# Fused window attention and gated FFN on one core: products with v in every third batch, a new order of the start, 30 heap slots

## The chip, the cores and the metric

The kernel runs on one core of one Trainium2 chip. The metric is the device time of the whole program in microseconds (us); lower is better. TensorE multiplies matrices, VectorE and ScalarE work element by element (both read PSUM), GpSimd works element by element on SBUF only, SyncE (SP) issues nearly all the DMAs.

## The reference

```python
xn = layernorm(x)                                  # x: 2048 tokens x 512
q, k, v = split(xn @ wqkv)                         # 32 heads of 16
scores = einsum("qd,kd->qk", q, k) * 16**-0.5
mask: 0 <= i - j < 256                             # causal, window of 256
o = softmax(scores, masked) @ v
s = o.reshape(S, D) @ wo
h = silu(xn @ w1) * (xn @ w3)                      # F = 1792
g = silu(h @ w2)
return x + s * g
```

All inputs are float32. The weights are large, so scores have a wide range, and the kernel carries about float32 accuracy through.

## The kernel before, in words

**Numbers.** A float32 matrix product is made of three float16 products: each operand is scaled by a power of two and cut into a high part (a cast) and a low part (the rest), and hi*hi + lo*hi + hi*lo is summed in PSUM. For tokens these parts are `XH` and `XL`; for weights `split` makes them (ScalarE the high part, VectorE the low) or `split_pool` (ScalarE twice, GpSimd the low part in two halves). The power of two of a weight comes from its sum of squares: `squares` adds them up per partition (on ScalarE for the first `on_act` parts, on VectorE for the rest; both write the squares themselves into a scratch tile that nobody reads), and `powers` sums over the partitions by a small matmul with ones and rounds on VectorE.

**Tiles and stages.** The tokens go in four tiles of 512 (`t`), the heads in four groups of eight (`g`). `prepare(0)` loads four blocks of x, takes mean and variance (`stats`), the inverse root by Newton steps (`rstd`), centres them, and turns each by four transposes on TensorE (`turn`: PSUM to XH by ScalarE, to XL by VectorE one step later). `project(t, g, k)` makes q (k = 0) or k (k = 1) for a group: twelve matmuls of 128x512 in two halves of six, then out to DRAM, from where `fetch` brings it back with one head to a strip of partitions. `value(j)` makes v for a block of 128 tokens.

**Attention** is done in 32 units `(t, g, p)`, four heads each. `pass1` makes the scores once with the queries on the partitions (L459) and takes the row maximum on VectorE (L464); at its end the maxima are turned on TensorE (L475), go to DRAM and come back as two more rows of the q operand. `pass2`, two units later in the order of the program, makes the scores again with the keys on the partitions (L506, maximum already subtracted), adds the masks on VectorE (L515, L520), takes the exponential on ScalarE into a tile `pt` (L524) and multiplies with v in float32 (L534; each such product appears as two instructions in the trace) into the one PSUM tile `po`. A unit has six chunks of keys and queries (five in the first tile).

**The order.** TensorE runs in the order in which the program is written; on the other engines a scheduler orders at compile time, and `tc.issue_after` keeps what is written in its block behind a given instruction of the same engine. `batches(u, ahead)` pairs the scores of unit u with the first pass of the unit two further on: seven batches of one or two score tiles. Products with v are not made with their scores but put on a list, `late`, and taken off in a later batch: `take_cols` says in which. `spread` puts dense work (FFN, projections, v, the output product) between the batches by matmul counts; `later(n, f)` runs f after n such steps. `flush` runs what is still queued. The FFN is written as a list of pieces (`feed_forward`): `load` brings raw weights, `measure` and `measure_down` scale and cut them during the first tile (cut weights are kept in DRAM and fetched again for later tiles), `gate_up` (L667) and `down` (L712) multiply.

**Memory.** Most passing tiles of 2 KB a partition are slots of one heap: `take` gives the slot that has been free longest, `give` puts it back, in program order; the writer of a slot waits for the last user of what was in it. The heap has 33 slots. PSUM has three buffers for dense results (`psm`), two double-size ones for scores (`pss`), one for `po`.

**The start** is written out by hand: fillers on TensorE (`keep_busy`), the statistics, the scale of the first q and k weights between the turns, then the projections of groups 0 and 1, v, and the scale and cut of the next weights between them. The fourth q and k weights are loaded (`qk[3][0]`) before the first unit, their squares are asked for after it (`qk[3][1]`), their scale three steps later.

**The end**: four calls of `total`, each the output product of 128 tokens (twelve matmuls), gated, added to x and stored.

Of the kernel before, what the change touches and what calls it, by code (L numbers as in the profile page):

```python
# [28 lines left out]
NT = 4  # L29
# [18 lines left out]
SLOTS = 33  # L48
# [13 lines left out]
def tile_block(ctx: ExitStack, tc: tile.TileContext, x, wqkv, wo, w1, w3, w2, out):  # L62
# [98 lines left out]
    ones = const.tile([4, KW], F16, name="ones")  # L161
# [6 lines left out]
    def squares(parts, on_act=0, apart=0):  # L168
# [4 lines left out]
        def one(i, raw):  # L173
            sq = take(BF16)
            if i < on_act:
                nc.scalar.activation(sq[:, 0:raw.shape[-1]], raw, AF.Square, accum_out=ssq[:, i:i + 1])
            else:
                nc.vector.tensor_tensor_reduce(out=sq[:, 0:raw.shape[-1]], in0=raw, in1=raw, scale=1.0, scalar=0.0,
                                               op0=ALU.mult, op1=ALU.add, accum_out=ssq[:, i:i + 1])
            give(sq)  # L180
# [35 lines left out]
    def split(hi, lo, raw, s):  # L216
        nc.scalar.activation(hi, raw, AF.Copy, scale=s)  # L217
# [16 lines left out]
    def weights(name, w):  # L234
# [8 lines left out]
        def norm(apart=0):  # L243
            cell["sb"] = squares(cell["raw"], on_act=4 * (name == "wv"), apart=apart)
# [22 lines left out]
    def weights_qk(g):  # L267
# [11 lines left out]
        def scale():  # L279
# [3 lines left out]
            cell["sw"] = scaled(inv, WS, f"sw{g}")  # L283

            cell["es"] = es = const.tile([P, 1], F32, name=f"es{g}")
            nc.vector.tensor_scalar(es, p2, p2, DH**-0.5 / QS**2, op0=ALU.mult, op1=ALU.mult)

        def cut():
            hi = const.tile([P, 2, NC, P], F16, name=f"whi{g}")
            lo = const.tile([P, 2, NC, P], F16, name=f"wlo{g}")  # L290
            for k, raw in enumerate(cell["raw"]):
                split(hi[:, k].rearrange("p c f -> p (c f)"), lo[:, k].rearrange("p c f -> p (c f)"), raw, cell["sw"])
            give(*cell["raw"])
            WQK[g] = hi, lo, cell["es"]
# [8 lines left out]
    def prepare(t):  # L303
# [3 lines left out]
        xts = {}  # L307

        def load(b):
            xts[b] = take(F32)  # L310
            nc.sync.dma_start(xts[b], x[t * TW + b * P:t * TW + (b + 1) * P, :])
# [20 lines left out]
        def centre(b):  # L332
            nc.vector.tensor_scalar(xts[b], xts[b], mv[:, b, 0:1], rs[:, b:b + 1], op0=ALU.subtract, op1=ALU.mult)

        def turn(b):
# [4 lines left out]
            pt = psm.tile([P, NC, P], F32, name="mm", tag="mm")  # L340
# [3 lines left out]
            with urgent():  # L344
                nc.scalar.copy(xh[:, :, c], pt)
# [48 lines left out]
    def project(t, g, k):  # L394
# [3 lines left out]
        def part(half):  # L398
# [3 lines left out]
            if half == 0:  # L402
                cell["pp"] = psm.tile([P, TW], F32, name="mm", tag="mm")
            for c in (2 * half, 2 * half + 1):
                for i, (a, b) in enumerate(((hi, xh), (lo, xh), (hi, xl))):
                    nc.tensor.matmul(cell["pp"], a[:, k, c, :], b[:, c, :], start=c == 0 and i == 0,  # L406
                                     stop=c == NC - 1 and i == 2)
            if half == 0:
# [20 lines left out]
        return [(6, lambda h=h: part(h)) for h in range(2)]  # L429
# [59 lines left out]
    def pass2(t, g, p):  # L489
# [6 lines left out]
        def scores(c):  # L496
# [25 lines left out]
            cell[c] = pt = ppool.tile([P, 4, 256], F32, name="pt")  # L522
# [85 lines left out]
    def measure(f, apart=0):  # L608

        raws = [RAW[f + i][0] for i in range(2)]  # L610
        sb = squares([raws[0][0], raws[1][0], raws[0][1], raws[1][1], RAW[f][1], RAW[f + 1][1]], on_act=6 if f == 0 else 4, apart=apart)
# [154 lines left out]

    def feed_forward():
# [47 lines left out]
    def batches(u, ahead):  # L815
# [10 lines left out]
        for k, pair in enumerate(pairs):  # L826
            take_cols = not ahead or (k and k % 2 == 0 if u else k == 1)
# [13 lines left out]
            made.append((COLS * 2 * take_cols if u else 0, batch))  # L841
# [30 lines left out]
    nc.vector.memset(ones, ONE)  # L872
# [46 lines left out]
    with tc.issue_after(lasts["cut"].ins):  # L919
# [108 lines left out]
```

## Time and profile before

| | us |
|---|---|
| median of 3 runs | 888.89 (888.86 to 893.99) |
| the profiled execution | 888.72 |
| its span, first to last instruction | 886.7 |
| TensorE busy | 851.2 (96%) |
| VectorE busy | 620.3 (70%) |
| ScalarE busy | 442.2 (50%) |
| GpSimd busy | 193.9 (22%) |
| mean granted TensorE clock | 0.993 |
| HBM traffic over the span | 118 GB/s |

PE is TensorE's matmuls, PEld its weight loads, DVE VectorE, ACT ScalarE, POOL GpSimd, SPq SyncE's queue. A row of the chain in time or of the timeline is: start, length, engine, line, operation, tile written <- tiles read, shapes, number merged, and in brackets the idle time of the engine before it with what ended it. A row of groups is: line, engine, operation, tiles, shapes, count | busy us, mean ns | idle us before, by what. A row of waits is: who waited for whom: us in total, times, longest. A row of stages is: window, length, busy us and count of each engine (PE, PEld, DVE, ACT, POOL), granted clock, DMA share, GB/s.

### The profile page before, as it was taken

How to read it: one execution, taken by the hardware profiler on the slowest of the kernel's cores; microseconds unless marked ns; L12 is line 12 of the kernel's file. 1: busy time of each engine (PE TensorE's matmuls, PEld its weight loads, DVE VectorE, ACT ScalarE, POOL GpSimd, SP SyncE). 2: the span in 40 equal slices, each digit the busy share in tenths (PEclk: the TensorE clock that was granted, in tenths of full speed). 3: DMA queues.
4: the chain of work that ended last, by engine and by line, in shares of the span. 5: the costliest groups of instructions: out<-in, count | busy, mean ns of one | idle time of the engine just before them, and what ended most of it. 6: DMA issues, size and time to landing. Idle time of an engine off the chain costs nothing.

```text
span 886.7 us, 20405 instructions
## 1 busy us (share of the span) xinstructions
PE 851.2 (96%) x7813; PEld 376.8 (42%) x7813; DVE 620.3 (70%) x1823; ACT 442.2 (50%) x657; POOL 193.9 (22%) x308
## 2 busy tenths in 40 slices
PE   8978998899999999999999999999999999999997
PEld 3433443444444444444444444444444444444443
DVE  6766967786767667778767776677667777676435
ACT  6776867473435444444444454444454444544521
POOL 1236236151111203111111111221111103131211
PEclk9999999999999999999999999999999999999999
DMA  9827734636643343451434334433442343422201
GB/s 289 240 85 231 225 112 128 209 109 196 167 132 84 102 125 96 131 158 52 145 102 119 106 91 131 131 102 90 136 123 59 107 133 114 116 92 85 63 11 57
DMA packets 94989, 110.51 MB, mean 125 GB/s; under 512 B 16956, under 2 KB 60076, under 8 KB 94892
## 3 DMA queue, kind: packets, MB, share of 16 engines
q1 hardware_dynamic: 94892, 109.21, 41.7%
q8 instruction: 61, 1.00, 0.5%
q14 instruction: 36, 0.29, 0.1%
HBM read 76.28 MB, written 28.57 MB: 118 GB/s over the span
## 4 chain that ended last, share of the span: by engine, by line
PE 65%; DVE 9%; issue 7%; DMA 6%; ACT 6%; SPq 4%; POOL 4%; POOLq 0%; DVEq 0%; ACTq 0%
PE mm L667 22%; PE mm L712 14%; PE po L534 8%; PE s L506 5%; PE mm L406 5%; PE mm L754 4%; PE s L459 3%; POOL slot L223 3%; DVE junk L464 3%; PE mm L380 3%; SPq L573 2%; ACT pt L524 1%; ACT slot L227 1%; DMA slot<-in_B_w_dram 1%; DMA dW<-slot 1%
## 5 line engine op out<-in xcount | busy, mean ns | idle before, releaser
L524 ACT ACTIVATE pt<-s,es 128x1024 f32<-128x1024 f32 (+1 forms) x184 | 200.8, 1093 | 233.0 <-DVE s L520 119.9
L667 PE MATMUL mm<-XH,slot 128*128 128x512 f16 x896 | 269.4, 382 | 2.1 <-DVE XL L350 1.2
L223 POOL TENSOR_TENSOR slot<-slot,slot 128x256 f16<-128x256 f32 (+1 forms) x220 | 147.4, 695 | 537.6 <-ACT slot L691 414.7
L464 DVE CUSTOM_DVE_ANT_0 junk<-s,MW 128x320 bf16<-128x320 f32 x448 | 217.8, 486 | 23.9 <-PE s L459 13.5
L667 PEld LDWEIGHTS <-slot 128*128 128x128 f16 x1344 | 122.0, 98 | 162.8 <-issue 32.2
L667 PE MATMUL mm<-XL,slot 128*128 128x512 f16 x448 | 170.8, 381 | 0.0
L712 PE MATMUL mm<-slot,slot 128*128 128x512 f16 x672 | 159.1, 380 | 0.3
L520 DVE TENSOR_TENSOR s<-s,M 128x512 f32<-128x512 f32 x128 | 89.0, 696 | 80.3 <-PE s L506 74.4
L534 PE MATMUL po<-pt,V 128*32 128x128 f32 (+1 forms) x1920 | 99.1, 333 | 0.0
L712 PEld LDWEIGHTS <-slot 128*128 128x128 f16 x672 | 60.7, 98 | 80.1 <-issue 12.9
L459 PE MATMUL s<-KA,qa 48*64 48x320 f16 (+2 forms) x1024 | 73.2, 297 | 11.4 <-DVE M L464 7.7
L506 PE MATMUL s<-qa,KA 50*64 50x128 f16 (+1 forms) x1920 | 74.2, 251 | 7.6 <-DVE M L464 4.6
L515 DVE TENSOR_TENSOR s<-s,M 128x1024 f32<-128x1024 f32 x56 | 68.8, 1228 | 17.0 <-PE s L506 14.7
L506 PEld LDWEIGHTS <-KA 50*64 50x64 f16 x1920 | 33.5, 105 | 82.3 <-issue 49.2
L682 DVE SCALAR_TENSOR_TENSOR slot<-slot,mm 128x512 f32<-128x512 f32 x56 | 38.4, 685 | 40.2 <-ACT slot L678 40.2
L691 ACT CAST slot<-slot 128x512 f16<-128x512 f32 x56 | 34.5, 616 | 54.5 <-DVE slot L687 54.5
L534 PEld LDWEIGHTS po<-pt,V 128*32 128x32 f32 x1920 | 50.2, 110 | 25.1 <-issue 12.4
L678 ACT ACTIVATE slot<-mm,sgs 128x512 f32<-128x512 f32 x56 | 38.2, 683 | 28.5 <-PE mm L667 28.2
L687 DVE SCALAR_TENSOR_TENSOR slot<-mm,slot 128x512 f32<-128x512 f32 x56 | 38.6, 689 | 18.7 <-PE mm L667 18.6
L728 DVE SCALAR_TENSOR_TENSOR slot<-mm,dsc,slot 128x512 f32<-128x512 f32 x48 | 35.9, 749 | 21.8 <-PE mm L712 21.7
L223 POOL TENSOR_TENSOR on<-on,rb 128x256 f32<-128x256 f32 x32 | 22.6, 727 | 126.5 <-DMA qa<-dm 92.5
L406 PE MATMUL mm<-XH,whi 128*128 128x512 f16 x128 | 49.2, 384 | 0.6 <-ACT whi L217 0.6
(111 smaller groups left out, 834.7 us busy)
## 6 DMA issues: line engine op xcount, KB each, us to landing
slot<-dW SPq DMA_DIRECT2D x126, 256.0 KB
slot<-in_B_w_dram SPq DMA_DIRECT2D x42, 256.0 KB
dW<-slot SPq DMA_DIRECT2D x42, 256.0 KB
slot<-in_A_x_dram SPq DMA_DIRECT2D x32, 256.0 KB
KA<-dK SPq DMA_DIRECT2D x24, 288.0 KB
qa<-dQ SPq DMA_DIRECT2D x32, 192.0 KB
dK<-slot SPq DMA_DIRECT2D x16, 256.0 KB
dQ<-slot SPq DMA_DIRECT2D x16, 256.0 KB
```

The costliest lines, as they stand in the source:

```text
L223: op(out[:, c], a[:, c], b[:, c])
L406: nc.tensor.matmul(cell["pp"], a[:, k, c, :], b[:, c, :], start=c == 0 and i == 0, stop=c == NC - 1 and i == 2)
L459: nc.tensor.matmul(s[64 * c:64 * c + 64, r, :n], qa[rows, 2 * p + a, ii * P + 64 * c:ii * P + 64 * c + 64], ka[rows, 2 * p + a, e - n:e], ...
L464: nc.vector.tensor_tensor_reduce(out=junk[:, :n], in0=s[:, r, :n], in1=mask, scale=1.0, scalar=NEG, op0=ALU.add, op1=ALU.max, accum_out=M[ ...
L506: nc.tensor.matmul(s[h:h + 64, r, o:o + w * P], ka[rows, 2 * p + a, (j + 2) * P + h:(j + 2) * P + h + 64], qa[rows, 2 * p + a, q * P:(q + ...
L515: nc.vector.tensor_add(sv, sv, m.unsqueeze(1).to_broadcast([P, 4, 2, P]))
L520: nc.vector.tensor_add(sv[:, :, b, :], sv[:, :, b, :], M2[:, k:k + 1, :].to_broadcast([P, 4, P]))
L524: nc.scalar.activation(pt[:, :, 0:n], s.rearrange("p r (a q) -> p (r a) q", a=2)[:, :, 0:n], AF.Exp, scale=es)
L534: nc.tensor.matmul(cell["po"][32 * i:32 * i + 32, q * P:(q + w) * P], V[:, (4 * t + j) % VB, h * VW:h * VW + 32], pt[:, i, o:o + w * P], s ...
L667: nc.tensor.matmul(cell[k], w[:, (a * NC + c) * P:(a * NC + c + 1) * P], b[:, c, :], start=c == 0 and i == 0, stop=c == NC - 1 and i == 2)
L687: nc.vector.scalar_tensor_tensor(sg, cell[1], 0.5 * HS / (WS * XS)**2, sg, op0=ALU.mult, op1=ALU.mult)
L712: nc.tensor.matmul(ps, hh[:, a * TW + b * P:a * TW + (b + 1) * P], w[:, c * D:(c + 1) * D], start=f == f0 and i == 0, stop=f == f1 - 1 and ...
```

## The change

- In `batches`, late products are taken in every third batch instead of every second; their share in `spread` is 9 instead of 6. `pt` has four buffers instead of three.
- The heap has 30 slots instead of 33. The scratch of `squares` is a pair of tiles of its own per engine, no longer a slot; the `ones` tile becomes a slot for the time that it is needed.
- Some squares move from ScalarE to VectorE (two of wv, two of `measure(0)`).
- The start: x is loaded on two queues (SP and ScalarE), the first tile is turned into the `pss` buffers, the first weights are scaled before the tokens are centred, cut k before q, and `project` can take its twelve products in another order: all of hi*hi first, lo*hi next, hi*XL last. 22 fillers, then 9, then 4, for 40 and 6. `issue_after` orders ScalarE and VectorE in more places.
- The squares of the fourth q and k weights are asked for six steps into the first unit.
- At the end the last 128 tokens go through `total_by_columns`: two halves of 256 columns, each stored by itself.

```diff
-SLOTS = 33
+SLOTS = 30
...
-    ones = const.tile([4, KW], F16, name="ones")
...
         def one(i, raw):
-            sq = take(BF16)
+            sq = ppool.tile([P, D], BF16, name="sqa" if i < on_act else "sqd", bufs=2)
...
-            give(sq)
...
-        nc.scalar.activation(hi, raw, AF.Copy, scale=s)
+        lasts["hi"] = nc.scalar.activation(hi, raw, AF.Copy, scale=s)
...
-            cell["sb"] = squares(cell["raw"], on_act=4 * (name == "wv"), apart=apart)
+            cell["sb"] = squares(cell["raw"], on_act=2 * (name == "wv"), apart=apart)
...
-        def cut():
...
+        def cut(ks=(1, 0)):
...
+            for k in ks:
+                raw = cell["raw"][k]
                 split(hi[:, k].rearrange("p c f -> p (c f)"), lo[:, k].rearrange("p c f -> p (c f)"), raw, cell["sw"])
+                give(raw)
...
-            nc.sync.dma_start(xts[b], x[t * TW + b * P:t * TW + (b + 1) * P, :])
+            (nc.scalar if t == 0 and b % 2 else nc.sync).dma_start(xts[b], x[t * TW + b * P:t * TW + (b + 1) * P, :])
...
-            pt = psm.tile([P, NC, P], F32, name="mm", tag="mm")
+            if t:
+                pt = psm.tile([P, NC, P], F32, name="mm", tag="mm")
+            else:
+
+                if b % 2 == 0:
+                    pair["s"] = pss.tile([P, 2, 512], F32, name="s")
+                pt = pair["s"][:, b % 2, :].rearrange("p (k q) -> p k q", q=P)
...
-    def project(t, g, k):
+    def project(t, g, k, terms=(range(3),)):
...
+        parts = ([[(c, i) for c in (2 * half, 2 * half + 1) for i in range(3)] for half in range(2)] if len(terms) == 1
+                 else [[(c, i) for i in group for c in range(NC)] for group in terms])
...
-            cell[c] = pt = ppool.tile([P, 4, 256], F32, name="pt")
+            cell[c] = pt = ppool.tile([P, 4, 256], F32, name="pt", bufs=4)
...
-        sb = squares([raws[0][0], ...], on_act=6 if f == 0 else 4, apart=apart)
+        sb = squares([raws[0][0], ...], on_act=4, apart=apart)
...
+    def total_by_columns(t, b):
...
+        for c in (slice(0, 256), slice(256, 512)):
+            ps = psm.tile([P, 256], F32, name="mm", tag="mm")
+            for g in range(NG):
+                for i, (a, w) in enumerate(((0, WOH), (0, WOL), (1, WOH))):
+                    nc.tensor.matmul(ps, O[t, g][:, a, tb], w[:, g, c], start=g == 0 and i == 0,
+                                     stop=g == NG - 1 and i == 2)
+            nc.vector.scalar_tensor_tensor(y[:, c], ps, sc["y"], y[:, c], op0=ALU.mult, op1=ALU.mult)
+            nc.vector.tensor_add(y[:, c], y[:, c], xr[:, c])
+            nc.sync.dma_start(out[r, c], y[:, c])
...
-            take_cols = not ahead or (k and k % 2 == 0 if u else k == 1)
+            take_cols = not ahead or (k and k % 3 == 0 if u else k == 1)
...
-            made.append((COLS * 2 * take_cols if u else 0, batch))
+            made.append((COLS * 3 * take_cols if u else 0, batch))
...
-    keep_busy(40)
+    keep_busy(22)
     for b in range(4):
         stats0(b)
     qk[0][1]()
+    qk[0][2]()
+    keep_busy(9)
     rstd0(0, 4)
     for b in range(4):
         centre0(b)
-    qk[1][1]()
+    with tc.issue_after(lasts["centre"].ins):
+        qk[0][3]((1,))
     for b in range(2):
         turn0(b)
-        step()
-    qk[0][2]()
+    step()
     for b in range(2, 4):
         turn0(b)
-        step()
-    keep_busy(6)
-    flush()
-    qk[0][3]()
-
-    k00 = project(0, 0, 1)
-    run(k00[:1])
-    wv[1]()
+    with tc.issue_after(lasts["xh"].ins):
+        qk[0][3]((0,))
+    with tc.issue_after(lasts["cut"].ins):
+        flush()
+    with tc.issue_after(lasts["hi"].ins), tc.issue_after(lasts["x"].ins):
+        qk[1][1]()
+        wv[1]()
+    keep_busy(4)
+
+
+    k00, q00 = (project(0, 0, k, ((0,), (1,), (2,))) for k in (1, 0))
+    run([k00[0], q00[0], k00[1], q00[1]])
     qk[1][2]()
-    run(k00[1:])
-    with tc.issue_after(lasts["cut"].ins):
-        qk[1][3]()
-    run(project(0, 0, 0))
+    qk[1][3]()
+    with tc.issue_after(lasts["hi"].ins):
+        run([k00[2], q00[2]])
+    later(1, lambda: fetch(0, 0))
+    k01 = project(0, 1, 1, ((0, 2), (1,)))
+    run(k01[:1])
     wv[2]()
-    later(1, lambda: fetch(0, 0))
-    run(project(0, 1, 1))
-    with tc.issue_after(lasts["cut"].ins):
+    with tc.issue_after(lasts["hi"].ins), tc.issue_after(lasts["cut"].ins):
         wv[3]()
-        sc["uv"] = scaled(SQ["wv"][2], 1.0 / (WS * XS), "uv")
-        sc["o"] = scaled(SQ["wv"][3], OS, "so")
+    run(k01[1:])
+    sc["uv"] = scaled(SQ["wv"][2], 1.0 / (WS * XS), "uv")
+    sc["o"] = scaled(SQ["wv"][3], OS, "so")
+    with tc.issue_after(lasts["hi"].ins):
         measure(0)
...
     started.append(True)
+    later(6, qk[3][1])
     spread(batches(None, units[0]), value(2) + value(3) + more(EARLY // 2))
-    qk[3][1]()
     later(3, qk[3][2])
...
-        run(total(NT - 1, b))
+        if b < 3:
+            run(total(NT - 1, b))
+    total_by_columns(NT - 1, 3)
     flush()
```

More of the change, by code (lines that the diff above doesn't have):

```diff
@@ L401, in part @@
             xh, xl = X[t]
-            if half == 0:
+            if n == 0:
                 cell["pp"] = psm.tile([P, TW], F32, name="mm", tag="mm")
[L404 to L408, printed above, removed]
+            for c, i in parts[n]:
+                a, b = ((hi, xh), (lo, xh), (hi, xl))[i]
+                nc.tensor.matmul(cell["pp"], a[:, k, c, :], b[:, c, :], start=(c, i) == parts[0][0],
+                                 stop=(c, i) == parts[-1][-1])
+            if n < len(parts) - 1:
                 return
@@ L428, in part @@
             later(1, rest)
-        return [(6, lambda h=h: part(h)) for h in range(2)]
+        return [(len(l), lambda n=n: part(n)) for n, l in enumerate(parts)]
     def fetch(t, g):
@@ L871, in tile_block @@
     wout = weights("wo", wo)
-    nc.vector.memset(ones, ONE)
+    ones = take(F16)
+    nc.vector.memset(ones[0:4, 0:KW], ONE)
     for b in range(4):
@@ L934, in tile_block @@
         for q in range(2):
[L935 removed]
+            nc.sync.dma_start(KA[r][64 * q + KR:64 * q + KR + 2], ones[2 * q:2 * q + 2, 0:KW].unsqueeze(1).to_broadcast([2, 4, KW]))
+    give(ones)
     qk[2][1]()
```

42 lines of the change are left out of this document (27 added, 15 removed).

## The prediction

> **What bounds the kernel now.** I read the page first, then the waits of TensorE, then a table of stages.
>
> ```profile
> PE 851.2 (96%) x7813; PEld 376.8 (42%) x7813; DVE 620.3 (70%) x1823; ACT 442.2 (50%) x657; POOL 193.9 (22%) x308
> PE ps L202 <- DVE sb L189: 5.4, 2, 5.1
> PE s L459 <- DVE M L464: 7.7, 11, 1.5
> PE s L506 <- DVE M L464: 4.6, 5, 2.7
> 0.00:18.10 18.10, 15.23 (x64) 6.94 (x64) 12.72 (x44) 10.84 (x26) 3.39 (x24) 1.00 0.97 285
> 18.10:53.60 35.50, 34.04 (x194) 15.05 (x195) 25.15 (x105) 24.60 (x53) 7.94 (x11) 1.00 0.78 221
> 53.60:58.90 5.30, 0.17 (x2) 0.02 (x1) 0.86 (x2) 5.30 (x12) 4.52 (x8) 0.93 0.22 74
> 58.90:100.00 41.10, 37.88 (x282) 15.70 (x282) 31.11 (x114) 31.43 (x61) 20.66 (x32) 0.93 0.61 189
> 100.00:150.00 50.00, 45.67 (x407) 20.77 (x406) 36.38 (x134) 37.00 (x68) 19.22 (x30) 0.97 0.47 142
> 150.00:200.00 50.00, 45.75 (x407) 20.07 (x405) 38.13 (x134) 31.23 (x54) 21.21 (x33) 1.00 0.53 158
> 600.00:700.00 100.00, 99.84 (x1015) 44.02 (x1004) 71.15 (x199) 44.68 (x56) 14.60 (x22) 1.00 0.38 109
> ```
>
> TensorE sets the end: 99.84 of 100 us in the window at 600. There a change pays only by taking time out of TensorE's own stream. What TensorE loses, it loses early: 18 us before the first projection (busy then with filler matmuls of L893), one hole of 5.3 us at 53.6, and 3.2 + 4.3 + 4.3 = 11.8 us between 58.9 and 200, where the waits are for VectorE. The columns after the five engines are the granted clock, the DMA share and GB/s. So the sum has a start, a hole, the early waits, the long dense middle, and a tail.
>
> **The start.** Now:
>
> ```profile
> 1.06 11.70 PE L893 MATMUL ps<-onesb 128*128 128x512 bf16 x40 [1.06 <-DVE onesb L136]
> 10.34 0.17 DVE L330 TENSOR_SCALAR rs<-r 128x4 f32<-128x4 f32 x1
> 11.53 1.00 DVE L333 TENSOR_SCALAR slot<-slot,mv,rs 128x512 f32<-128x512 f32 x2
> 12.59 1.04 PE L342 MATMUL mm<-identf,slot 128*128 128x128 f32 x8
> 15.57 0.63 PE L342 MATMUL mm<-identf,slot 128*128 128x128 f32 x4 [1.00 <-DVE XL L350]
> 16.24 0.58 ACT L345 CAST XH<-mm 128x512 f16<-128x512 f32 x1
> 16.86 0.69 DVE L350 TENSOR_TENSOR XL<-mm,XH 128x512 f16<-128x512 f32 x1 [0.17 <-ACT XH L345]
> 18.11 0.39 PE L406 MATMUL mm<-XH,whi 128*128 128x512 f16 x1 [0.56 <-ACT whi L217]
> 18.95 0.39 PE L406 MATMUL mm<-XH,wlo 128*128 128x512 f16 x1 [0.45 <-DVE wlo L218]
> ```
>
> The stream of projections is unbroken from 18.95, so it stands as if begun at 18.7. Centring ends at 12.53, but the last transposed tile reaches XH only at 16.82: forty fillers, the scale of the weights between the turns, and a PSUM buffer that waits for XL (the 1.00 at 15.57) hold the transposes back. The new order scales the first weights before centring (a cast and six small operations of about 0.16, so centring ends near 13.3), turns into the two larger PSUM tiles, so that no turn waits for XL, and asks for all eight XH-whi products first, then eight with wlo, then eight with XL. Last turn about 0.5 (half of 1.04) and XH 0.58: first product near 14.3. XL (four of 0.69) and wlo (two such) take VectorE to about 17.4; the sixteen products ahead of XL last 16 x 0.22 (the L712 row further down has six in 1.47 with the last one's drain), 3.5 us, so XL is wanted at 17.8 and is there. Gross gain 4.4. Against it: the second weights' scale and measure(0) keep their places behind the projections, their squares now run later (behind XH and whi), so I take back 1.4 for waits. Half the x loads go on ScalarE's queue, past SP's; the DMA share is 0.97 in this stage, so the bytes bind, and I give that nothing. Squares moved from ScalarE to VectorE (two of wv, two of measure(0), at 0.62 + 0.19 against 0.69 + 0.08) hide in a stage where both are 70% busy. **3.0**, bounds -1.0 (all waits come back, and one more) and 4.6.
>
> **The hole at 53.6.**
>
> ```profile
> 57.28 0.63 ACT L176 ACTIVATE slot<-slot 128x512 bf16<-128x512 f32 x1
> 58.66 0.17 DVE L189 CAST sb<-ssq 128x2 bf16<-128x2 f32 x1 [2.80 <-ACT slot L176]
> 58.88 0.19 PE L202 MATMUL ps<-sb,onesb 128*128 128x1 bf16 x2 [5.13 <-DVE sb L189]
> 56.00:58.00 2.00, 0.00 (x0) 0.00 (x0) 0.00 (x0) 2.00 (x6) 1.81 (x4) 1.00 0.59 196
> 58.00:60.00 2.00, 1.12 (x5) 0.46 (x5) 0.96 (x7) 1.85 (x5) 0.76 (x2) 0.53 0.00 1
> 60.00:62.00 2.00, 2.00 (x13) 0.52 (x11) 1.21 (x3) 1.93 (x5) 0.00 (x0) 0.61 0.00 0
> ```
>
> The squares of the fourth q and k weights stand behind a full ScalarE queue, and TensorE, in program order, waits 5.13 us for their sum. Afterwards the granted clock is 0.53 and 0.61 for four us: (0.47 + 0.39) x 2 = 1.7 us more. The change calls qk[3][1] six steps into the first unit instead of after it, some 8 us earlier, while its scale keeps its place. The hole is worth 6.8. ScalarE is full from 53.6 to 62, so part of its backlog will be late for the next user, the FFN weights. I take **5.5**, bounds 0 and 6.8.
>
> On the same rows: the Trainium skill, page "TensorE: Matmul & The Clock Gate", section "Part 1: The HAM clock gate", says that an idle window of about 3.4 us halves the clock until a busy one has passed; the trace agrees (0.53 after 5.1 us). The rule speaks against the change at the start, where fillers fall from forty to 22 and 9 with a wait between; that is a rival below.
>
> **Squares and the heap.**
>
> ```profile
> 130.83 7.23 POOL L223 TENSOR_TENSOR slot<-slot,slot 128x256 f16<-128x256 f32 x10 [1.30 <-ACT slot L227]
> 134.68 1.14 DVE L178 CUSTOM_DVE_ANT_0 slot<-slot 128x512 bf16<-128x512 f32 x1 [2.37 <-POOL slot L223]
> 136.09 0.41 PE L506 MATMUL s<-qa,KA 50*64 50x256 f16 x8 [2.67 <-DVE M L464]
> DVE slot L178 <- POOL slot L223: 5.0, 3, 2.4
> ACT slot L227 <- POOL slot L223: 4.1, 4, 1.5
> L176 ACT ACTIVATE slot<-slot 128x512 bf16<-128x512 f32 x42 | 26.1, 622 | 8.9 <-DMA slot<-in_A_wqkv_dram 6.3 <-POOL slot L223 2.4
> L178 DVE CUSTOM_DVE_ANT_0 slot<-slot 128x512 bf16<-128x512 f32 x16 | 11.4, 715 | 5.0 <-POOL slot L223 5.0
> ```
>
> A square writes a scratch result that nobody reads, into a heap slot, and waits until GpSimd has done with that slot; behind it stand VectorE's maxima, and behind those TensorE: 2.37 became 2.67, and with a slow clock like that above 4.4 us. With scratch tiles of its own this goes. The price is three slots. Following take and give through the code, the free list is never shorter than 3 after a take now, so 0 after the change; but the 42 + 16 squares no longer take slots. Takes whose slot was given back fewer than 40 matmuls before number 24 now and 23 then: 12 against 16 up to about 115 us, 12 against 7 after it; past 200 us none has fewer than 90. (The ones tile, now a slot too, is given back before the list gets short.) So the reserve is no worse on the whole, somewhat worse in the second unit, and I book **3.5** of the 4.4; bounds 6.7 (all 5.0 and the clock) and -18 (rival three).
>
> **The products with v.**
>
> ```profile
> 609.48 1.08 PE L534 MATMUL po<-pt,V 128*32 128x256 f32 x24
> 610.49 1.47 PE L712 MATMUL mm<-slot,slot 128*128 128x512 f16 x6
> 152.72 0.43 PE L534 MATMUL po<-pt,V 128*32 128x128 f32 x8
> 153.07 1.47 PE L712 MATMUL mm<-slot,slot 128*128 128x512 f16 x6
> ```
>
> Start to start, a run of two chunks (24 instructions, 512 columns a head; the row names only its first shape) lasts 1.01, one of a single chunk (8, 128 columns) 0.35. That is 0.66/384 = 1.72 ns a column and 0.35 - 0.22 = 0.13 us for a run, whatever its length. A unit has seven batches; runs stand at batches 2, 4, 6 now, at 3 and 6 after. Thirty units lose one run: 30 x 0.13 = **3.9**, bounds 0 (the 0.13 belongs to the neighbours) and 4.5 (0.15 a run). A run of three chunks should take 1.42. The newest chunk in a run is still that of the batch before, so its exponential is as early as now; the fourth pt holds the chunk made meanwhile. The transposed maxima leave one batch later (a seventh of a unit, which lasts about 26 us: 32 of them in the span after 45), with four batches left before their reader. The dense work per unit is shared out as before (two shares of 9 for three of 6).
>
> **The tail.**
>
> ```profile
> 882.17 0.75 DVE L758 SCALAR_TENSOR_TENSOR slot<-mm,us,slot 128x512 f32<-128x512 f32 x1 [1.11 <-PE mm L754]
> 882.96 0.69 DVE L760 TENSOR_TENSOR slot<-slot,slot 128x512 f32<-128x512 f32 x1
> L464 DVE CUSTOM_DVE_ANT_0 junk<-s,M 128x256 bf16<-128x256 f32 x32 | 13.4, 419 | 0.7
> ```
>
> The last block in two halves leaves only a half behind the last product: two operations near 0.42 instead of 0.75 + 0.69, so **0.6**; bounds -0.3 (twelve more matmuls and a second store) and 1.0 (the store is shorter too).
>
> **Sum.** 3.0 + 5.5 + 3.5 + 3.9 + 0.6 = 16.5. The profiled execution took 888.72, span 886.7 and 2.0 around it; that gives 872.2, and the median shown lies 0.17 above that execution. I say 872.
>
> **Rivals.** *One, the gain stays:* nothing moves into the gaps, the start is taken whole and the early waits shrink with the squares: 4.4 + 6.8 + 6.0 + 4.2 + 0.8 = 22.2, so 866. For it: ScalarE and VectorE are free a quarter of the time there. Against: the waits for L464 come in eleven and five places, not in one. Chance 0.20. *Two, the wall moves:* TensorE arrives earlier and meets ScalarE's backlog of weight cuts (5.30 busy of 5.30 in the hole); start and hole are given back, 3.5 + 3.9 + 0.6 = 8.0 stay: 881. Chance 0.15. *Three, slower:* with an empty free list in the second unit, writes by ScalarE and VectorE stand behind GpSimd's subtractions as the square at 134.68 did, 4.4 us each time. Four new ones eat the sum; from there it is a loss, and six cost 26: 898. Against: the count of close takes. Chance 0.05. *Four, the clock at the start:* fillers end near 8.8 (22 at up to 0.43 while the clock is low) and the sum of squares may wait on VectorE behind the chain that ends at 10.51; then the transposes and first products run at half clock and cost the same 1.7 again: 874. The skill's clock-gate page gives it its reason. Chance 0.10. The forecast has 0.50.
>
> **How the numbers follow.** One per cent, about what a measurement here tells from no change, is 8.9 us: faster means under 880, slower over 898. Forecast, rivals one and four lie under 880 but for 0.03; rival two lies about the line, 0.07 under; rival three is half over. Faster 0.84, same 0.13, slower 0.03. The range goes from 859 (rival one, and half of the other early waits) to 885 (rival two with no gain from the squares).
>
> **What would show it.** Groups of L534 of 32 instructions lasting 1.42, some 60 of them; first L406 near 14.3; no TensorE wait on L189 over 1 us; no L178 wait on GpSimd; last L758 on 256 columns near 0.42. I am wrong if the first L406 comes after 17, if a hole of over 3 us stands between 40 and 75, if waits on L223 exceed the 11 us now, or if windows after 300 us lose what their runs gain.

## The result, and the profile after

The changed kernel takes 900.27 us (median of 4 runs, 899.55 to 901.50) against 889.33 us for the kernel before on the same chip: a ratio of 1.0122, with an interval of 1.0102 to 1.0142. It is 11 us slower where 17 us of gain were predicted. Its profiled execution took 899.55 us, with a span of 897.6. Most line numbers have moved: L421 is the projection (L406 before), L474 and L521 the scores of the two passes (L459, L506), L479 the maxima (L464), L539 the exponential (L524), L549 the products with v (L534), L353 the transposes (L342), L682 the first FFN products (L667) and L693 their tanh (L678), L200 and L187 the sum of squares and its cast (L202, L189), L221 GpSimd's subtractions (L223).

First the page's line of busy times and the waits of TensorE in the changed kernel (microseconds in total, times, longest):

```profile
PE 845.8 (94%) x7814; PEld 382.9 (43%) x7814; DVE 624.9 (70%) x1833; ACT 440.7 (49%) x649; POOL 192.3 (21%) x308
PE s L474 <- DVE M L479: 14.0, 24, 1.3
PE ps L200 <- DVE sb L187: 7.4, 3, 5.3
PE s L521 <- DVE M L479: 5.8, 11, 1.8
PE s L474 <- ACT pt L539: 5.1, 4, 3.6
PE mm L353 <- DVE slot L697: 3.6, 1, 3.6
PE mm L682 <- DVE slot L434: 2.8, 1, 2.8
```

TensorE is busy for 5.4 us less than before, and the span is 10.9 us longer. The waits for the maxima have grown from 12.3 us in 16 places to 19.8 in 35, and three waits of about 3 us have appeared that the kernel before does not have. The same windows as before show where they lie:

```profile
0.00:18.10 18.10, 14.14 (x64) 6.74 (x65) 12.33 (x43) 8.07 (x18) 3.39 (x24) 1.00 0.97 289
18.10:53.60 35.50, 27.23 (x154) 11.57 (x152) 23.55 (x88) 24.66 (x58) 7.66 (x10) 0.94 0.84 234
53.60:58.90 5.30, 5.30 (x26) 2.05 (x25) 4.98 (x30) 4.42 (x9) 1.99 (x4) 0.76 0.00 0
58.90:100.00 41.10, 34.88 (x260) 14.80 (x259) 29.65 (x109) 28.86 (x54) 20.19 (x32) 0.96 0.51 168
100.00:150.00 50.00, 41.41 (x334) 18.12 (x332) 33.21 (x112) 32.85 (x59) 17.89 (x28) 0.93 0.49 149
600.00:700.00 100.00, 97.11 (x1003) 43.79 (x996) 69.84 (x199) 42.00 (x53) 14.57 (x22) 1.00 0.40 108
```

The window at 53.6 is now full, but the one ahead of it has lost 6.8 us of TensorE's work (34.04 before): the hole has moved, not gone. Between 58.9 and 150 TensorE idles for 14.8 us, against 7.6 before. And the window at 600, where only 0.16 us in 100 were idle, now loses 2.9.

**The start.** TensorE's rows, in order of time:

```profile
12.63 1.09 PE L353 MATMUL s<-identf,slot 128*128 128x128 f32 x8 [0.68 <-ACT XH L356]
15.81 1.89 PE L421 MATMUL mm<-XH,whi 128*128 128x512 f16 x8
22.44 1.04 PE L421 MATMUL mm<-XH,whi 128*128 128x512 f16 x4 [1.24 <-ACT whi L215]
31.39 0.17 PE L200 MATMUL ps<-sb,onesb 128*128 128x6 bf16 x1 [0.60 <-DVE sb L187]
```

The first product comes at 15.81, 2.3 us earlier than before and 1.5 later than predicted: the transposes no longer wait for XL, but twice for XH (0.68 ahead of 12.63, 0.73 ahead of 14.45). Then TensorE waits 1.24 for the second weights, and 0.60 for measure(0): what the start has won goes back into such waits. The tanh of the first FFN block (L693) starts at 44.66, where its counterpart of before (L678) starts 0.4 later.

**The hole.** TensorE again, and below it rows of ScalarE's stream:

```profile
52.53 0.17 PE L200 MATMUL ps<-sb,onesb 128*128 128x6 bf16 x1 [5.32 <-DVE sb L187]
53.31 1.04 PE L682 MATMUL mm<-XH,slot 128*128 128x512 f16 x2
...
44.66 0.69 ACT L693 ACTIVATE slot<-mm,sgs 128x512 f32<-128x512 f32 x1 [3.38 <-PE mm L682]
47.97 0.62 ACT L706 CAST slot<-slot 128x512 f16<-128x512 f32 x1 [2.63 <-DVE slot L702]
48.50 0.62 ACT L175 ACTIVATE sqa<-slot 128x512 bf16<-128x512 f32 x1
```

The sum waited for has 6 columns: these are the squares of FFN weights 2 and 3, and no longer those of the fourth q and k weights. In the kernel before they ran at 29.5 to 32.3. Now ScalarE idles twice (3.38 and 2.63), and only from 48.50 does it do nine squares in a row, the two of the fourth q and k weights ahead of the four that TensorE wants. The two matmuls of L682 after it take 1.04 instead of 0.60: half clock, as in the hole before.

**The heap.** VectorE and ScalarE between 88 and 150, with two loads as SyncE issues them:

```profile
91.17 0.69 DVE L319 BATCH_NORM_STATS2 st<-slot 128x6 f32<-128x512 f32 x1 [2.67 <-DMA slot<-in_A_x_dram]
96.26 0.33 PE L474 MATMUL s<-KA,qa 48*64 48x320 f16 x4 [3.56 <-ACT pt L539]
88.05 0.92 SPq L315 DMA_DIRECT2D slot<-in_A_x_dram  x2
122.13 7.23 SPq L617 DMA_DIRECT2D slot<-in_B_w_dram  x3
133.60 0.94 DVE L177 CUSTOM_DVE_ANT_0 sqd<-slot 128x512 bf16<-128x512 f32 x1 [2.21 <-DMA slot<-in_B_w_dram]
134.03 0.60 ACT L430 ACTIVATE slot<-mm 128x512 f16<-128x512 f32 x1 [1.70 <-POOL slot L221]
135.40 1.01 PE L682 MATMUL mm<-XH,slot 128*128 128x512 f16 x2 [2.83 <-DVE slot L434]
143.38 0.69 ACT L693 ACTIVATE slot<-mm,sgs 128x512 f32<-128x512 f32 x1 [1.40 <-POOL slot L221]
144.84 1.12 PE L353 MATMUL mm<-identf,slot 128*128 128x128 f32 x4 [3.62 <-DVE slot L697]
```

Behind the first of TensorE's three long waits (3.56, 2.83 and 3.62) is a load: the statistics of x stand on VectorE ahead of the maxima, are wanted at 88.50, and their tile was asked for only at 88.05. That this wait is the heap's is not shown: the kernel before asks for the same tiles at 89.72, and its statistics, from 94.75 on, do not wait. At 122.13 three loads of FFN weights take SyncE 7.23 us to issue, for it waits between them for the last users of their slots (in the kernel before two take 4.99 at 116.14). The load behind them (L619), issued only at 130.25, is the one that VectorE's square waits for. Behind the second wait are that load and a slot, which end together: the square at 133.60 and ScalarE's write at 134.03, which waits for GpSimd to be done with what it writes over. Behind the third is a slot alone, that of the tanh at 143.38.

**The runs of three.** Two neighbouring batches of one unit in the dense stage, TensorE alone:

```profile
622.71 0.47 PE L474 MATMUL s<-KA,qa 48*64 48x320 f16 x8
623.11 1.51 PE L549 MATMUL po<-pt,V 128*32 128x128 f32 x32
624.56 0.42 PE L521 MATMUL s<-qa,KA 50*64 50x128 f16 x16
625.79 0.33 PE L474 MATMUL s<-KA,qa 48*64 48x320 f16 x4 [0.81 <-PE s L521]
```

The run lasts 1.45, as computed. But right behind it come the next scores, with no dense piece between; the scores fill their buffers and TensorE stands still for 0.81 of the 1.23 us from 624.56 to 625.79 (the sixteen of L521 take 0.25 elsewhere). The run counts as 9 matmuls in spread, which is 1.94 us at 0.216 each, so its batch has had its share and gets nothing.

### The profile page after: what moved, and what is told of

Read it like the earlier page. It is cut to its first block, busy times and chain, and to the rows that moved or that the text cites. A ratio compares the mean times of both kernels' runs of the same rounds, so it can differ in the third digit from the quotient of the medians.

```text
span 897.6 us, 20451 instructions
## 1 busy us (share of the span) xinstructions
PE 845.8 (94%) x7814; PEld 382.9 (43%) x7814; DVE 624.9 (70%) x1833; ACT 440.7 (49%) x649; POOL 192.3 (21%) x308
## 4 chain that ended last, share of the span: by engine, by line
PE 69%; DVE 12%; issue 5%; ACT 5%; DMA 5%; POOL 3%; SPq 1%; POOLq 0%; DVEq 0%; ACTq 0%
PE mm L682 26%; PE mm L727 14%; PE mm L421 7%; PE s L521 5%; DVE junk L479 5%; PE po L549 5%; PE mm L769 4%; PE s L474 4%; PE mm L391 3%; POOL slot L221 3%; DMA slot<-in_B_w_dram 2%; DMA slot<-in_A_x_dram 1%; DVE slot L697 1%; DVE s L530 1%; ACT slot L224 1%
## 5 line engine op out<-in xcount | busy, mean ns | idle before, releaser
L539 ACT ACTIVATE pt<-s,es 128x1024 f32<-128x1024 f32 (+1 forms) x184 | 201.1, 1094 | 197.4 <-DVE s L535 124.9
L682 PE MATMUL mm<-XH,slot 128*128 128x512 f16 x896 | 270.4, 384 | 3.2 <-DVE slot L434 2.8
L221 POOL TENSOR_TENSOR slot<-slot,slot 128x256 f16<-128x256 f32 (+1 forms) x220 | 146.0, 691 | 555.1 <-ACT slot L706 408.7
L479 DVE CUSTOM_DVE_ANT_0 junk<-s,MW 128x320 bf16<-128x320 f32 x448 | 218.0, 487 | 32.1 <-PE s L474 21.5
L682 PEld LDWEIGHTS <-slot 128*128 128x128 f16 x1344 | 124.4, 98 | 161.9 <-issue 23.2
L682 PE MATMUL mm<-XL,slot 128*128 128x512 f16 x448 | 171.2, 382 | 0.0
L727 PEld LDWEIGHTS <-slot 128*128 128x128 f16 x672 | 61.8, 98 | 80.7 <-issue 11.7
L474 PE MATMUL s<-KA,qa 48*64 48x320 f16 (+2 forms) x1024 | 73.9, 300 | 20.9 <-DVE M L479 14.0
L549 PE MATMUL po<-pt,V 128*32 128x128 f32 (+1 forms) x1920 | 92.0, 329 | 0.0
L521 PE MATMUL s<-qa,KA 50*64 50x128 f16 (+1 forms) x1920 | 74.7, 252 | 6.8 <-DVE M L479 5.8
L521 PEld LDWEIGHTS <-KA 50*64 50x64 f16 x1920 | 33.3, 105 | 80.0 <-issue 44.5
L549 PEld LDWEIGHTS po<-pt,V 128*32 128x32 f32 x1920 | 52.0, 109 | 18.8 <-issue 6.9
L693 ACT ACTIVATE slot<-mm,sgs 128x512 f32<-128x512 f32 x56 | 38.2, 683 | 33.9 <-PE mm L682 32.1
L474 PEld LDWEIGHTS <-qa 48*64 48x64 f16 x1024 | 28.7, 106 | 52.1 <-issue 30.1
L221 POOL TENSOR_TENSOR on<-on,rb 128x256 f32<-128x256 f32 x32 | 22.6, 726 | 120.8 <-DMA dm<-mt 110.4
```

Of the source, the lines that this page charges most:

```text
L221: op(out[:, c], a[:, c], b[:, c])
L474: nc.tensor.matmul(s[64 * c:64 * c + 64, r, :n], qa[rows, 2 * p + a, ii * P + 64 * c:ii * P + 64 * c + 64], ka[rows, 2 * p + a, e - n:e], ...
L479: nc.vector.tensor_tensor_reduce(out=junk[:, :n], in0=s[:, r, :n], in1=mask, scale=1.0, scalar=NEG, op0=ALU.add, op1=ALU.max, accum_out=M[ ...
L521: nc.tensor.matmul(s[h:h + 64, r, o:o + w * P], ka[rows, 2 * p + a, (j + 2) * P + h:(j + 2) * P + h + 64], qa[rows, 2 * p + a, q * P:(q + ...
L539: nc.scalar.activation(pt[:, :, 0:n], s.rearrange("p r (a q) -> p (r a) q", a=2)[:, :, 0:n], AF.Exp, scale=es)
L549: nc.tensor.matmul(cell["po"][32 * i:32 * i + 32, q * P:(q + w) * P], V[:, (4 * t + j) % VB, h * VW:h * VW + 32], pt[:, i, o:o + w * P], s ...
```

## The experiments

Three theories, in the order of the stages: A, the early qk[3][1] moved the hole; B, the weight of 9 and not the grouping costs time in the dense stage; C, 30 slots are too few. Ratios are to the kernel before on the same chip in the same comparison (its median there lay between 889.0 and 891.6).

**The parts of the change undone.** Runs q9, pairs, pairs_32 and before_30:

```
q9         later(6, qk[3][1])            ->  later(9, qk[3][1])
pairs      k % 3, COLS * 3               ->  k % 2, COLS * 2
pairs_32   as pairs, pt bufs=4, SLOTS 30 ->  pt bufs=3, SLOTS 32
before_30  (before) SLOTS 33             ->  SLOTS 30
```

> The kernel after, with qk[3][1] called nine steps into the first unit instead of six, which is behind the call that measures FFN weights 2 and 3 and no longer ahead of it. Theory A (the early call put the squares of those FFN weights behind squares whose load is still on its way, and so moved the hole from 58.7 to 52.5): ScalarE's squares of slots for FFN weights 2 and 3 run before 48, TensorE's wait of 5.32 us on L187 near 52 falls under 1 us, no wait over 1.5 us stands between 40 and 75, and the whole is 5 to 7 us shorter: 893 to 896. Rival (ScalarE's backlog in this stage makes a hole wherever the squares stand): a wait of 3 to 6 us on L187 between 45 and 65, and 899 to 902.

> The kernel after, with the products with v at every second batch again, two chunks at once (weight 6); four weight tiles and 30 slots stay. Theory B (a run of three leaves the batch behind it without dense work, and TensorE then waits for the maxima, which costs more than the 0.13 us saved per run left out): TensorE's waits on L479 fall from 20 us to under 10, the windows from 200 to 830 become about 5 us shorter, and the whole is 894 to 897. Rival (the saving is real and the waits come from the heap or from the maxima themselves): the waits on L479 stay near 20 us and the whole is 903 to 906, for 30 runs of 0.13 to 0.15 come back.

> As pairs, with three weight tiles instead of four, and the room given to the heap: 32 slots. Theory C (30 slots make loads of x and of FFN weights start late, and writes wait for GpSimd; this is what is lost between 90 and 150): against pairs 4 to 6 us less, so 888 to 893; first waits on DMA of L177 and L319 between 90 and 150 gone, and ScalarE's and VectorE's waits on L221 back under 5 us. Rival (the slots lost do nothing; the scratch tiles and the order of squares make the stalls): within 1.5 us of pairs, with the same waits between 90 and 150.

> The kernel before with 30 slots in the heap instead of 33, nothing else. Theory C: 5 to 10 us slower, 894 to 899, with late loads and waits for GpSimd between 58 and 150 that the kernel before does not have (there the squares still take slots too, so it may be more than in the change). Rival (slots are no limit): 888 to 890.

Measured: q9 904.52 (1.0145, 1.0106 to 1.0184); pairs 897.27 (1.0084, 1.0053 to 1.0115); pairs_32 886.61 (0.9961, 0.9942 to 0.9979); before_30 898.40 (1.0094, 1.0060 to 1.0127).

**C holds.** Two slots more, with one weight tile fewer, turn 1.0084 into 0.9961, 10.9 us; three slots fewer and nothing else cost the kernel before 8.4. The pair also separates the stages: windows of TensorE's busy time in before_30, and then in pairs_32.

```profile
100.00:150.00 50.00, 39.19 (x342) 17.54 (x340) 30.54 (x109) 29.63 (x55) 14.56 (x23) 0.93 0.45 138
600.00:700.00 100.00, 99.57 (x1008) 43.71 (x1007) 72.63 (x205) 44.30 (x55) 15.97 (x24) 1.00 0.40 110
...
100.00:150.00 50.00, 44.63 (x408) 20.11 (x404) 37.27 (x135) 36.62 (x66) 18.57 (x30) 1.00 0.45 136
```

With 30 slots the kernel before loses 6.5 us of TensorE's work between 100 and 150 (45.67 there with 33) and 0.3 in the window at 600; with 32 the changed kernel in pairs does 44.63 between 100 and 150, at full clock. Not all went as expected: the waits of VectorE and ScalarE for loads between 85 and 150 fall from 13.0 us in pairs to 8.1 in pairs_32, but do not vanish.

The run pairs, against the change, tells of B only in part. It is some 3 us faster, and from the fifth to the last unit its span is 4.7 us shorter, but TensorE still waits 16.1 us for the maxima, where under 10 were expected.

**A holds in part only.** In q9 the squares of FFN weights 2 and 3 ran before 47, but their cast stood on VectorE behind that of the fourth q and k weights, and a wait of 2.95 stayed at 56.68. The whole was slower than the change, in part for a reason of its own. TensorE at the start of q9, and a row of stages for TensorE alone (its busy time, granted clock, DMA share, GB/s):

```profile
9.40 0.19 PE L200 MATMUL ps<-sb,onesb 128*128 128x1 bf16 x2 [2.03 <-DVE sb L187]
...
12.02 1.06 PE L353 MATMUL s<-identf,slot 128*128 128x128 f32 x4
19.01 2.87 PE L421 MATMUL mm<-XH,whi 128*128 128x512 f16 x8
...
10.00:20.00 10.00, 8.65 (x31) 0.54 1.15 318
```

The first product comes at 19.01 instead of 15.81, since the clock has halved behind the filler matmuls: rival four of the prediction, in this execution. That is 3.2 of the 8.2 us by which this execution, the longest of q9's four, exceeds the change's; the rest is lost up to the third unit, and its cause is open.

**The weight, the slots above 32, the start, the order.** Runs weight_2 (the change with COLS * 2 for a run of three) and base_33 with two variants:

```
base_33       after: k % 2, COLS * 2; pt bufs=3; sqa and sqd bufs=1; SLOTS 33
base_33_fill  base_33: keep_busy(22) -> keep_busy(28)
base_33_q10   base_33: later(6, qk[3][1]) -> later(10, qk[3][1])
```

> The kernel after, where a run of three chunks is counted with 6 matmuls of dense work instead of 9 in the sharing-out; runs, tiles and heap stay as in the change. Theory B, first form (the batch with the run gets no dense piece, and TensorE waits for the maxima of VectorE): the waits on L479 fall from 20 us to 10 or less, the drift of 6 us between unit 7 and unit 30 goes, and the whole is 894 to 896. Second form (TensorE loses there because of the run itself, three chunks in a row, whatever stands beside it): the waits stay at 15 us or more and the whole is 899 to 901.

> The kernel after with the products with v in pairs, three weight tiles, one scratch tile for each engine's squares instead of two, and the room given to the heap: 33 slots, as many as the kernel before has, while the squares take none. Theory C (a slot is worth 3 to 5 us from 30 to 32, with less to win above): 883 to 887. Rival (32 were enough): as pairs_32, 886 to 887; or the single scratch tile chains the squares and costs 1 to 3 us: 888 to 890.

> base_33 with 28 filler matmuls ahead of the first sum of squares instead of 22. Theory D (the wait of 1.5 to 2.0 us before that sum is near the length at which the clock drops, so that in some executions the transposes and first products run at half clock and 3 to 6 us are lost): the wait ahead of the first L200 falls under 0.6 us, the granted clock is 1.00 up to 20 us in the profile, and the times spread by less than 2 us, with a median 1 to 2 us below base_33. Rival (the spread has nothing to do with the start): same median within 0.5 us and the same spread of 5 us.

> base_33 with qk[3][1] ten steps into the first unit instead of six: squares and cast of FFN weights 2 and 3 are then ahead of those of the fourth q and k weights on both ScalarE and VectorE (nine steps had put only the squares ahead, and 2.95 us of the hole were left behind the cast). Theory A: no TensorE wait over 1.5 us on L187 between 40 and 75, and 3 to 5 us less than base_33: 879 to 883. Rival (the hole comes back at the scale of the fourth weights near 58, as in the kernel before): a wait of 3 to 5 us there and the time of base_33 within 1.5 us.

Measured: weight_2 893.04 (1.0021, 0.9998 to 1.0045); base_33 888.90 (0.9983, 0.9966 to 1.0001); base_33_fill 890.68 (1.0008, 0.9990 to 1.0026); base_33_q10 886.32 (0.9952, 0.9930 to 0.9974).

**B holds.** Nothing but the weight takes 9.0 us (1.0122 to 1.0021) off the change. TensorE's waits in weight_2:

```profile
PE s L474 <- DVE M L479: 4.9, 11, 1.0
PE s L521 <- DVE M L479: 3.4, 7, 1.6
```

19.8 us have become 8.3 (its profiled execution, 889.07, was the shortest of ten). The 33rd slot gave nothing that shows: base_33 lies 2 us above pairs_32, with intervals that overlap, and the single scratch tile that came with the slot was not tried alone. More fillers gave nothing either: with the wait gone the times still spread by 4.7 us (3.4 in base_33), and theory D falls. base_33_q10 gained 2.6 us, but not as A had it:

```profile
60.02 0.19 PE L200 MATMUL ps<-sb,onesb 128*128 128x1 bf16 x2 [5.12 <-DVE sb L187]
```

The hole (6.03 at 54.41 in base_33) is where it was in the kernel before, at the scale of the fourth q and k weights. In the orders tried, whichever of the two sets of squares stands first leaves the other late.

**The parts one by one on the kernel before, and all of them mended.** Runs before_three, three_32_q10, three_31_q10, pairs_32_q10:

```
before_three   (before) k % 2 -> k % 3; COLS * 2, pt bufs=3 and SLOTS 33 stay
three_32_q10   after: COLS * 2; pt bufs=3; SLOTS 32; later(10, qk[3][1])
three_31_q10   after: COLS * 2; sqa and sqd bufs=1; SLOTS 31; later(10, qk[3][1])
pairs_32_q10   pairs_32: later(10, qk[3][1])
```

> The kernel before, with the products with v at every third batch and the weight of a run left at 6 matmuls; three weight tiles, 33 slots, nothing else. Theory B (the grouping itself saves a run of 0.13 to 0.2 us a unit, and only the weight of 9 and the heap spoil it): 4 to 6 us faster than before, 884 to 886, all of it between unit 2 and unit 31. Rival (with three weight tiles the fourth exponential has to wait for the run, the scores behind it wait for a PSUM buffer, and that costs what the run saves): waits of TensorE on the exponential (L524) rise from near nothing to over 6 us, and 889 to 893.

> The change with a weight of 6 for a run of three, three weight tiles and so 32 slots, and qk[3][1] ten steps into the first unit. If heap (30 to 32 slots: 10.7), weight and order add up: pairs_32's 886.6, less 5 for the grouping, less 2.6 for the order: 877 to 881. Rival (as with before_three, three tiles are too few for runs of three): 885 to 889.

> The same with four weight tiles, one scratch tile for each engine's squares, and so 31 slots. Theory C says that 31 slots still cost half of what 30 cost against 32, 3 to 6 us: 881 to 886. Rival (the loss sits wholly between 30 and 31): 877 to 881, as three_32_q10.

> pairs_32 with qk[3][1] ten steps into the first unit. If what it gave base_33 (2.6 us) holds here: 883 to 885. Rival (it only made good what the single scratch tile had cost there): 886 to 887, as pairs_32.

Measured: before_three 876.27 (0.9839, 0.9816 to 0.9863); three_32_q10 879.60 (0.9876, 0.9855 to 0.9898); three_31_q10 891.42 (1.0005, 0.9991 to 1.0019); pairs_32_q10 883.19 (0.9922, 0.9898 to 0.9946).

One character of the change, the grouping alone, gains 14.4 us (12.7 between the two profiled executions) and beats all of it together. Beside the other edits it gains far less: three_32_q10 and pairs_32_q10 differ in the grouping alone, and lie 3.6 us apart. Three weight tiles are enough: TensorE's waits in before_three, with the run that has its dense work again:

```profile
PE s L506 <- DVE M L464: 5.2, 9, 1.4
PE s L459 <- DVE M L464: 3.8, 8, 0.7
PE s L506 <- ACT pt L524: 1.8, 3, 1.1
...
603.48 1.51 PE L534 MATMUL po<-pt,V 128*32 128x128 f32 x32
604.92 0.39 PE L754 MATMUL mm<-woh,O 128*128 128x512 f16 x1
```

Between three_31_q10 and three_32_q10 lie 11.5 us (1.0005 against 0.9876), more than either expectation allowed. They differ by one slot, but also in the scratch tiles (one for each engine against two) and the weight tiles (four against three). Between the two profiled executions 8.0 us are lost by the third copy of a unit's result, 1.2 of them by the first copy, the others in the stage where 30 slots cost most (below). So it is likely, but not shown, that the heap's price comes as a step. And three_32_q10, the change with weight, heap and order mended, gets 22 us back (1.0122 to 0.9876), about what the three gave one by one (9.0, 10.9 and 2.6), yet stays above before_three. In pairs, what is left of the other edits (start, order, scratch tiles, tail) gains 6.9 us, as pairs_32_q10 against before shows; on top of the grouping they gain nothing, with one slot fewer. In the profiles three_32_q10 loses some 4 us against before_three between the third unit and the eleventh; the cause is open.

**What each mistake costs by itself.** On before_three, the weight of 9 (before_w9), the 30 slots (before_three_30), the tail (before_three_tail); and the smaller sum of weights without the grouping (before_pairs_w4):

```
before_w9          before_three: COLS * 2 -> COLS * 3
before_pairs_w4    (before) COLS * 2 -> 4, pairs stay
before_three_30    before_three: SLOTS 33 -> 30
before_three_tail  before_three: the last block by total_by_columns
```

> before_three (the kernel before with runs of three, 33 slots) with the weight of a run at 9 instead of 6, as the change has it. If the weight leaves the batch with the run without dense work also here: a drift of 8 to 12 us against before_three between unit 4 and unit 31, TensorE's waits on L464 above 15 us against 9.0, and 884 to 890 against 876.3. Rival (the drift in the change came from its four weight tiles or its heap): within 2 us of before_three.

> The kernel before, in pairs, with the weight of a run at 4 instead of 6: the weights of a unit sum to 12, as in before_three. If the 15 us of before_three come from the sharing-out alone: 877 to 882. If they are the grouping's (fewer runs, and scores that come without a run between them): 888 to 892, the time of the kernel before.

> before_three with 30 slots instead of 33. If the heap's price is the same with the grouping as without (8.4 us from before to before_30): 883 to 887, all of it lost before 200 us. Rival (the grouping spreads the takes, and 30 slots do): 876 to 879.

> before_three with the last block in two halves of columns (total_by_columns), nothing else. The prediction's tail term says 0.6 less, bounds -0.3 and 1.0: 875.3 to 876.6. Rival (twelve more matmuls and a store more eat it): 876.3 to 877.

Measured: before_w9 892.54 (1.0026, 1.0010 to 1.0042); before_pairs_w4 890.97 (1.0014, 1.0003 to 1.0025); before_three_30 892.40 (1.0029, 1.0016 to 1.0041); before_three_tail 876.03 (0.9846, 0.9824 to 0.9869).

Either mistake alone eats the whole gain: 0.9839 goes to 1.0026 by the weight (16.6 us) and to 1.0029 by the heap (16.9 us). Both came out worse than expected (884 to 890 and 883 to 887), the heap twice as dear as without the grouping. The gain is the grouping's, for the sharing-out alone gives nothing. How the losses lie differs. The copy of each unit's result, 32 of them, first and last start, in before, before_three, before_w9 and before_three_30:

```profile
L542 ACT COPY os<-po x32: 566/585/587, 100.5 to 852.0; 128x512 f32<-128x512 f32 x32
...
L542 ACT COPY os<-po x32: 563/585/585, 100.4 to 839.3; 128x512 f32<-128x512 f32 x32
...
L542 ACT COPY os<-po x32: 565/585/586, 101.7 to 857.9; 128x512 f32<-128x512 f32 x32
...
L542 ACT COPY os<-po x32: 563/585/586, 100.0 to 855.6; 128x512 f32<-128x512 f32 x32
```

From first to last: 751.5, 738.9, 756.2, 755.6. The weight loses its 17 us bit by bit over the whole run of units, 4 of them between the copies at 713 and 741; the heap has lost 12.8 us by the third copy and 15.0 by the fourth, near 190. Most of it goes in one stage of before_three_30, with the same chain as behind the third wait in the change, only longer:

```profile
100.00:150.00 50.00, 37.74 (x299) 16.64 (x299) 29.91 (x103) 27.90 (x51) 14.52 (x22) 0.90 0.42 133
127.69 7.59 POOL L223 TENSOR_TENSOR slot<-slot,slot 128x256 f16<-128x256 f32 x12 [7.52 <-ACT slot L227]
143.60 0.69 ACT L678 ACTIVATE slot<-mm,sgs 128x512 f32<-128x512 f32 x1 [1.41 <-POOL slot L223]
145.07 1.12 PE L342 MATMUL mm<-identf,slot 128*128 128x128 f32 x4 [6.33 <-DVE slot L682]
```

37.74 us of work in 50 against 46.21 in before_three. GpSimd has twelve subtractions to do at once; ScalarE waits for it five times between 132 and 144, 5.5 us in all, the last time for the slot of the tanh; VectorE's product waits for the tanh, and TensorE 6.33 us for that.

## Why the prediction was wrong

**Squares and the heap: the step that failed first.** The prediction counted takes whose slot had been given back fewer than 40 matmuls before, found 23 against 24, and called the reserve no worse. That count has no time in it and does not see the queues: a take that waits in SyncE's order holds back every load behind it (7.23 us for three issues at 122.13), and one slot late on GpSimd holds ScalarE, VectorE and TensorE in turn. The wait that was to go did go: no square waits for GpSimd in the change. But booked were 3.5 of gain, and 30 slots for 33 or 32 cost 8 to 17 us. Rival three had the mechanism and its place, with a chance of 0.05. That its 898 lies near the measured 900 is luck: it put 26 us on the heap and kept all other gains, while here the heap cost 10.9, the weight 9.0, and start and hole gave next to nothing. The row that should have raised it was quoted: the 2.37 us wait at 134.68 was a slot's, in the kernel with 33 of them. The prediction took it for a price of the squares.

**The products with v: right in the run, wrong beside it.** The run of three lasts 1.45; predicted was 1.42, though the prediction's own figures (0.13 and 768 columns at 1.72 ns) make 1.45. The sentence that the dense work "is shared out as before (two shares of 9 for three of 6)" compared the sums, 18 and 18, and never asked what the one batch gets that is charged 9. There the step broke: 9.0 us in the change, 16.6 by itself. With the weight at 6 the grouping gives the mended change 3.6 us, near the 3.9 that were said, but the kernel before 14.4. From unit 14 to unit 31 of before_three the gain is 2.6 us, 0.15 a unit, as computed for a run; the rest falls where TensorE used to wait, between 100 and 450, 6.4 us of it by 175. The term left it out since it counted the run's own price alone. Which of fewer runs, later transposed maxima, or moved dense pieces takes those waits away was not separated; the sharing-out alone does not. That the other edits take away some of the same waits, and so leave the grouping less to gain, is likely, not shown.

**The hole: 5.5 booked, nothing got.** The prediction named ScalarE's backlog and expected the next user to be late by part of it. The next user was the FFN weights' own sum, late by all of it: 5.13 us at 58.88 became 5.32 at 52.53. In base_33_q10 it is 5.12 at 60.02. That is rival two for this stage.

**The start: 3.0 booked.** 2.3 us at the first product, 0.4 left at 45. The 1.4 taken back for waits should have been nearly the whole. Rival four was real in two of the profiled executions, in that of q9 and, for some 4 us, in that of three_31_q10.

**The tail: right.** From the last unit's copy to the end 34.7 us before, 34.2 in the change, 0.5 for a predicted 0.6; in before_three_tail the gain is too small for the interval.

Of the prediction's own marks, two spoke: a hole of over 3 us between 40 and 75, and windows after 300 that lose what their runs gain. Two did not: the first product came before 17, and the waits on GpSimd, to be wrong above 11 us, were some 8 (3.4 and 1.4 for L225 and L693, 1.7 for L430, 1.4 for L763). That mark sees only waits for slots and no loads: between 85 and 150 VectorE and ScalarE wait 13.3 us for loads in the change, and not at all in the kernel before.

## What to carry to other kernels

A scheduler's cost table is part of the kernel: when work is regrouped, work out for each batch what it will be given, not only that the sums agree. A pool of buffers shared by loads and by slow engines can cost more than it seems to hold in reserve, so a change that takes slots from it needs the waits and the load issues of the tightest stage read, not a count of reuses. And where several edits come together, the one with a clear row behind it is worth trying alone: here the grouping alone stood at 0.9839 and all of them at 1.0122. What an edit gains alone it need not gain beside others: 14.4 us became 3.6.

## What was not expected of the hardware

Whether a short wait at the start halves the clock cannot be read from its length. In q9 a wait of 2.03 us ahead of L200 was followed by 10 us at a granted clock of 0.54; in base_33_q10 a longer one was not, for the first transposes take 0.60 there as at full clock (in three_31_q10, after 2.39 us, they take 1.06):

```profile
9.62 0.19 PE L200 MATMUL ps<-sb,onesb 128*128 128x1 bf16 x2 [2.11 <-DVE sb L187]
...
11.61 0.60 PE L353 MATMUL s<-identf,slot 128*128 128x128 f32 x4
```

The Trainium skill, page "TensorE: Matmul & The Clock Gate", section "Part 1: The HAM clock gate", says that activity is judged in windows that run free of the kernel's start. The two rows agree with that: the same wait can fall inside one window in one execution and over two in another. But 2.03 us is shorter than the idle window of about 3.4 us that the prediction quotes from the same section, so a wait of full window length was not needed in q9; the measurement decides. No run here shows the windows themselves.
